# Second-half loads on ScalarE's queue, and a longer planned time for P's turn, in an attention and MLP kernel

## Chip, cores and metric

The kernel runs on one core of a Trainium2 chip. The metric is the device time of one execution in microseconds (us). A core has five engines that run side by side, each through a fixed list of instructions in order: TensorE (PE: matmuls), VectorE (DVE), ScalarE (ACT), GpSimd (POOL) and SyncE (SP), which here only issues DMAs. They meet through semaphores. 16 DMA engines move the data that any of them asks for.

## What is computed

Causal attention with a decay per head (4 batches, 8 heads, 576 positions, head width 64), then two MLPs on the 2,304 tokens (width 512; inner widths 2,048 and 1,536), all in float32:

```
scores = scale * np.matmul(q, k.transpose(0, 1, 3, 2))
cum = np.cumsum(np.log(np.clip(f, 0.0001, 1.0)), axis=-1)
scores = np.where(causal, -1000000000.0, scores + cum[:, :, :, None] - cum[:, :, None, :])
attn = np.exp(scores - np.max(scores, axis=-1, keepdims=True))
attn = attn / (np.sum(attn, axis=-1, keepdims=True) + 1e-09)
x = np.matmul(attn, v)        # then (tokens, 512)
r = np.maximum(x @ w_in, 0.0)
x = (r * r) @ w_out
g = x @ w_gate
out = (g * (1.0 / (1.0 + np.exp(-g))) * (x @ w_val)) @ w_out2
```

## The kernel before

**How the work is cut.** Precision comes from splitting each operand into a high and a low part and adding three (in the MLPs) or two matmuls. The attention runs in units: one unit is a batch `b` and a pair of heads `pr`, and does a half of the query rows (`attn_unit`, L343). The first half (`half` 0, "early") has the query rows 0 to 255 of all 16 units, in two tiles of 128 rows; the second half has rows 256 to 575 in three tiles, `i` = 4 (64 rows of both heads together), 3 and 2. Keys go up to 256 in the first half and to 576 in the second. The tokens of the first half make the MLP's token tiles 0 to 3 (256 tokens each, one for each batch), those of the second half tiles 4 to 8, laid end to end: 320 tokens a batch, so that tile 7 takes tokens of the batches 2 and 3, and tile 8 of batch 3 alone (`segments`, L869).

**A unit.** DMAs load K (`load_k`, L377), Q, V and the decay sums (`load_bias`, L395, broadcast to 128 partitions). ScalarE and VectorE split K and Q into parts (L402 to L418). For each tile and head (or both heads) TensorE makes the scores (L535), GpSimd masks the diagonal of the decay (L523), VectorE subtracts the decay and takes the row's extreme (`soft`, L558), ScalarE exponentiates (L576), and VectorE (with ScalarE for one of the two heads) writes P's high and low part as fp16 (L605 to L611). Then SyncE issues *P's turn* (`turn`, L628 to L636): a transposing DMA (L633) that writes P with keys on the partitions. n = `ng * 2 * nb` blocks of 128 x 128 are turned: 10, 16 and 12 in the second half's tiles, 8 and 4 in the first half's. The value matmuls (`mix`, L649) read the turned P, ScalarE scales and keeps the result (L675), and the unit's rows are stored (L692).

**Buffers.** In the second half, K's load has one buffer (`kr`), the decay has one in each of two sets that alternate between units, P has two (`P16`) and the turned P two (`PT`). The first half has three of P and three of the turned P.

**The order of the work.** A planner (class `Plan`, L47) writes the order of each engine by hand. Every step has an engine, an estimated time, steps that it waits for, buffers that it takes and a priority. `Plan.order` (L65) runs the steps through a model: each engine starts the ready step of the smallest priority number whose buffers are free. An attention step has the priority 10 x the number of its unit, a matmul of an MLP 500 and up, and the MLP's steps on ScalarE, VectorE and GpSimd -100; so TensorE does attention when it can and MLP matmuls otherwise. The order found this way is what each engine runs on the chip; times on the chip don't change it. For a step on SyncE the model adds a transfer: 290,000 bytes for each us on one shared channel, then 1.8 us until it has landed (L103 to L106). P's turn stands in it with 1.4 us of issue and 250,000 bytes whatever its size (L636).

```
                if e == SP:
                    free[e] = now + st.us
                    dma_free = max(free[e], dma_free) + st.nbytes / DMA_RATE
                    st.done = dma_free + DMA_LATENCY
```

**Stages.** The first half of the attention runs beside the loading and splitting of the first MLP's weights and its token tiles 0 and 1; the second half beside the tiles 2 to 6 of the first MLP as they come free; then follow the rest of the first MLP (`mlp_pair`, L771, with `first`, L736, and `second`, L744) and the second MLP (`mlp_wide`, L999). All DMAs, loads, turns and stores, are issued by SyncE on one queue.

Of the kernel before, what the change touches and what calls it, by code (L numbers as in the profile page):

```python
# [10 lines left out]
F16 = mybir.dt.float16  # L11
# [6 lines left out]
PE, ACT, DVE, POOL, SP = "PE", "ACT", "DVE", "POOL", "SP"  # L18
AFTER = {PE: 0.25, ACT: 0.2, DVE: 0.15, POOL: 0.2, SP: 0.0, None: 0.0}
DMA_ISSUE = 0.45  # L20
DMA_LATENCY = 1.8
DMA_RATE = 290e3
LAG1 = 2
GATE = 1
PACE = 4
LAG2 = 1

# [19 lines left out]
class Plan:  # L47
# [6 lines left out]
        first.next.append((then, False))  # L54


    def add(self, eng, us, fn, deps=(), pri=0, take=(), use=(), nbytes=0, order=()):
        deps, order = ([d for d in ds if d is not None] for ds in (deps, order))
        st = Step(len(self.steps), eng, us, fn, deps, order, pri, take, nbytes)
        for buf in (*take, *use):  # L60
            buf.users.append(st)
        self.steps.append(st)
        return st

    def order(self):  # L65
        now, dma_free = 0.0, 0.0
        free = {e: 0.0 for e in AFTER}
        cands = {e: [] for e in AFTER}
        rings, events, left = {}, [], len(self.steps)

        def fits(st):
            more = {}
            for buf in st.take:
                ring = rings.setdefault(buf.tag, [])
                at = len(ring) + more.get(buf.tag, 0) - buf.n
                more[buf.tag] = more.get(buf.tag, 0) + 1
                if at >= 0:
                    for u in ring[at].users:
                        if u.start is None or u.done > now:
                            return False  # L80
            return True

        for st in self.steps:
            if not st.left:
                cands[st.eng].append(st)
        while left:
            moved = False
            for e in free:
                if free[e] > now and e is not None:
                    continue  # L90
                best = None
                for st in cands[e]:
                    if st.ready <= now and (best is None or (st.pri, st.idx) < (best.pri, best.idx)) and fits(st):
                        best = st
                if best is None:
                    continue
                moved, st = True, best
                cands[e].remove(st)
                left -= 1
                st.start = now  # L100
                for buf in st.take:
                    rings[buf.tag].append(buf)
                if e == SP:  # L103
                    free[e] = now + st.us
                    dma_free = max(free[e], dma_free) + st.nbytes / DMA_RATE
                    st.done = dma_free + DMA_LATENCY  # L106
                else:
                    free[e] = now + st.us
                    st.done = now + st.us + AFTER[e]
                heapq.heappush(events, free[e])  # L110
                heapq.heappush(events, st.done)
                for nx, wait in st.next:
                    nx.left -= 1
                    nx.ready = max(nx.ready, st.done if wait else st.start)
                    if not nx.left:
                        cands[nx.eng].append(nx)
            if moved:
                continue
            while events and events[0] <= now:
                heapq.heappop(events)  # L120
            if not events:
                stuck = [st for e in cands for st in cands[e]]
                raise RuntimeError(f"the plan is stuck at {now}: {[(s.eng, s.pri, s.fn, [b.tag for b in s.take]) for s in stuck[:8]]}")
            now = heapq.heappop(events)
        return sorted(self.steps, key=lambda st: (st.start, st.idx))
# [22 lines left out]
def decay_attention_moe_kernel(ctx: ExitStack, tc, q, k, v, f, w1, w2, wg, wv, wo, outT):  # L148
    nc = tc.nc
    P = 128  # L150
# [36 lines left out]
    add = plan.add  # L187
# [36 lines left out]
    decayed = add(SP, DMA_ISSUE, lambda: nc.sync.dma_start(cum_d, fc[0]), [o3], -10, use=[fc_buf], nbytes=74000)  # L224
# [118 lines left out]
    def attn_unit(idx, b, pr, half, opened):  # L343
# [16 lines left out]
        c = {}  # L360
        x_buf = c["xbuf"] = XBUF[b] if early else None

        def take(eng, us, fn, deps, bufs, use=(), nbytes=0, p=pri):
            st = add(eng, us, fn, [*deps, opened], p, take=bufs, use=use, nbytes=nbytes,
                     order=[prev(x.tag) for x in bufs])
            for x in bufs:
                alloc_chain[x.tag] = st
            return st
# [8 lines left out]
        def load_k():  # L377
            if early:
                c["kr"] = h0.tile([P, 2, SPLIT], F32, tag="qk", bufs=3, name="kr")
            else:  # L380
                c["kr"] = pool().tile([P, 2, S], F32, tag="kr", name="kr")[:, :, :kmax]
            nc.sync.dma_start(c["kr"], k[b, h2, :, :kmax].rearrange("h d s -> d h s"))

        cols = slice(pr * P, pr * P + P)

# [9 lines left out]
        def load_bias():  # L395
            c["bias"] = kq_pool().tile([P, 2, kw], F32, tag="bias", bufs=nbuf, name="bias")
            r0 = b * H + 2 * pr
            nc.sync.dma_start(
                c["bias"][:, :, :kmax], cum_d[r0 : r0 + 2, :kmax].partition_broadcast(P)
            )  # L400

# [19 lines left out]
            (Buf("qk", 3), Buf("qk", 3)) if early else (Buf("kr", 1), Buf("qr", 1))  # L421
        ) + (Buf(tg + "vr", nbuf), Buf(kt + "bias", nbuf))
        KA, QA = Buf(kt + "KA", nbuf), Buf(kt + "QA", nbuf)
        lk = take(SP, DMA_ISSUE, load_k, [], [kr], nbytes=P * 8 * kmax)
        lq = take(SP, DMA_ISSUE, load_q, [], [qr], nbytes=P * 8 * qn)
        lb = BIAS[idx] = take(SP, DMA_ISSUE, load_bias, [decayed], [bias], nbytes=P * 8 * kmax)
        lv = take(SP, DMA_ISSUE, load_v, [], [vr], nbytes=P * 4 * 512)
        lv2 = add(SP, DMA_ISSUE, load_v2, [lv], pri, use=[vr], nbytes=32000)
        lv3 = add(POOL, 0.27, lambda: nc.gpsimd.memset(c["vr"][64:128, TAIL, :], 0.0), [lv], pri, use=[vr])
# [71 lines left out]
        for ti, i in enumerate(tiles):  # L501
# [86 lines left out]
                nc.vector.reciprocal(cg[:, :, 3], cg[:, :, 3])  # L588

            sm = add(DVE, 0.32, sums, exps, pri, use=[cg_buf])  # L590
            p_buf, t_buf = Buf(tg + "P16", 3 if early else 2), Buf(tg + "PT", 3 if early else 2)
            lows, pad = [], None
            for g in range(ng):
                on_act = early or g == 1

                def view(st=st, g=g, ng=ng, nb=nb):
                    return st["p16"].rearrange("p (g a n) -> p g a n", g=ng, a=2)[:, g]

                def p_hi(st=st, g=g, ng=ng, nb=nb, ext=ext, on_act=on_act, view=view):
                    if g == 0:  # L600
                        p16 = pool().tile([P, (8 if early else 16) * P], F16, tag="P16", bufs=3 if early else 2, name="p16")
                        st["p16"] = p16[:, : ng * 2 * nb * P]
                    cg, s, pv = st["cg"][:, g], st["s", g], view()
                    if on_act:
                        nc.scalar.activation(pv[:, 0, :ext], s[:, :ext], AF.Copy, scale=cg[:, 3:4])  # L605
                    else:
                        nc.vector.tensor_scalar(pv[:, 0, :ext], s[:, :ext], cg[:, 3:4], None, op0=ALU.mult)

                def p_lo(st=st, g=g, ext=ext, view=view):
                    cg, s, pv = st["cg"][:, g], st["s", g], view()  # L610
                    nc.vector.scalar_tensor_tensor(  # L611
                        pv[:, 1, :ext], s[:, :ext], cg[:, 3:4], pv[:, 0, :ext],
                        op0=ALU.mult, op1=ALU.subtract,
                    )

                eng, us = (ACT, act_us(ext)) if on_act else (DVE, dve1_us(ext))
                if g == 0:
                    first_hi = ph = take(eng, us, p_hi, [sm], [p_buf], use=[sbufs[g], cg_buf])
                else:
                    ph = add(eng, us, p_hi, [sm, first_hi], pri, use=[p_buf, sbufs[g], cg_buf])  # L620
                lows.append(add(DVE, dve_us(ext), p_lo, [ph], pri, use=[p_buf, sbufs[g], cg_buf]))
                if ext < nb * P:
                    lows.append(add(
                        POOL, 0.3, lambda view=view, ext=ext: nc.gpsimd.memset(view()[:, :, ext:], 0.0),
                        [ph], pri, use=[p_buf],
                    ))

            def turn(st=st, ng=ng, nb=nb):  # L628
                PT = pool().tile(
                    [P, (8 if early else 16) * P], F16, tag="PT", bufs=3 if early else 2, name="PT"  # L630
                ).rearrange("p (n q) -> p n q", q=P)
                n = ng * 2 * nb
                nc.sync.dma_start_transpose(out=PT[:, :n, :], in_=st["p16"])  # L633
                st["PT"] = PT[:, :n, :].rearrange("p (g a b) q -> p g a b q", g=ng, a=2)

            tn = take(SP, 1.4, turn, lows, [t_buf], use=[p_buf], nbytes=250000)  # L636


            def mix(ps, st=st, i=i, nb=nb, w=w):
# [539 lines left out]
```

## Time and profile before

| | us |
|---|---|
| median of 3 runs | 1107.16 (1103.6 to 1111.46) |
| the profiled execution | 1107.47 |
| its span, first to last instruction | 1105.7 |
| TensorE busy | 1028.4 |
| VectorE busy | 568.3 |
| ScalarE busy | 548.8 |
| GpSimd busy | 250.9 |

The profile is of one execution. An engine counts as busy while an instruction of its own runs on it; issuing a DMA, waiting and branching are not counted. "PE" is TensorE's matmuls and "PEld" its weight loads, which overlap them. Matmuls overlap one another, so a row's duration is longer than the distance to the next. "PEclk" is the share of TensorE's full clock (2.4 GHz) that was granted; 0.50 is the lower level, 1.2 GHz. A wait is named by who waited and by what ended it; "DMA PT<-p" is the landing of a turn of P. For a DMA, "to landing" is the time from the start of its issue until its data is there.

### The profile page before, as it was taken

To read this page: it belongs to the slowest core of one execution; us is meant where nothing else is said; L and a number is where in the kernel's file an instruction comes from. 1 tells how busy PE (TensorE), PEld (TensorE's weight loads), DVE (VectorE), ACT (ScalarE), POOL (GpSimd) and SP (SyncE) were. 2 spreads that over 40 slices of the span, in tenths; PEclk is the share of its full clock that TensorE was granted. 3 is DMA by queue.
4 is the path that set the end of the run, shared out by engine and by line. 5 is a ranking of instruction groups with operands and counts; after the bars stand their busy time and mean duration, and the time that the engine had idled before them with its cause. 6 is when DMAs were issued, how large, how long until landed. Compare 5 with 4: busy or idle time off the path is not lost.

```text
span 1105.7 us, 20516 instructions
## 1 busy us (share of the span) xinstructions
PE 1028.4 (93%) x7936; PEld 924.7 (84%) x7936; DVE 568.3 (51%) x1239; ACT 548.8 (50%) x1104; POOL 250.9 (23%) x341
## 2 busy tenths in 40 slices
PE   2567999999889998989999999999999999999998
PEld 2457999998889888979999998888888888888897
DVE  7889988537668878767371899102002000100010
ACT  6877888756556666756573887112112111211111
POOL 1232432332223223222122211111111111111111
PEclk9997999999889999989999999999999999999999
DMA  9978357459798979776561555002001100100010
GB/s 322 259 163 253 100 153 172 77 153 213 169 196 207 201 184 225 164 169 125 150 198 43 160 167 180 0 1 77 1 1 29 48 1 1 39 1 1 1 39 20
DMA packets 177922, 128.89 MB, mean 117 GB/s; under 512 B 110944, under 2 KB 164704, under 8 KB 176032
## 3 DMA queue, kind: packets, MB, share of 16 engines
q1 hardware_dynamic: 177824, 127.58, 45.2%
q8 instruction: 62, 1.02, 0.4%
q14 instruction: 36, 0.29, 0.1%
HBM read 89.20 MB, written 12.13 MB: 92 GB/s over the span
## 4 chain that ended last, share of the span: by engine, by line
PE 79%; DMA 10%; DVE 7%; issue 2%; ACT 2%; POOL 0%; SPq 0%; POOLq 0%; DVEq 0%; ACTq 0%
PE hp L739 29%; PE acc L747 16%; PE vp L739 14%; PE acc L1058 12%; DMA PT<-p 9%; PE ps L649 4%; PE ps L535 4%; DVE p L611 1%; DVE s L558 1%; DVE ct L270 1%; DVE ct L276 1%; DVE QB L410 1%; DMA raw<-in_moe_w_in_dram 1%; DVE wl_i L285 1%; DVE ct L266 0%
## 5 line engine op out<-in xcount | busy, mean ns | idle before, releaser
L1030 DVE TENSOR_TENSOR tmp<-tmp,vp 128x512 f32<-128x512 f32 x48 | 33.0, 687 | 301.9 <-PE vp L739 301.9
L825 POOL TENSOR_TENSOR gl<-tmp,gh 128x512 fp32r<-128x512 f32 x78 | 113.8, 1459 | 295.2 <-ACT gh L822 287.5
L739 PE MATMUL hp<-xh,wh_i 128*128 128x256 f32 x576 | 168.4, 292 | 0.0
L747 PE MATMUL acc<-gh,wh_o 128*128 128x256 f32 x576 | 166.1, 288 | 0.0
L739 PE MATMUL hp<-xl,wh_i 128*128 128x256 f32 x576 | 165.5, 287 | 0.0
L739 PE MATMUL hp<-xh,wl_i 128*128 128x256 f32 x576 | 165.2, 287 | 0.0
L747 PE MATMUL acc<-gh,wl_o 128*128 128x256 f32 x576 | 164.0, 285 | 1.2 <-DVE wl_o L285 1.2
L747 PE MATMUL acc<-gl,wh_o 128*128 128x256 f32 x576 | 164.1, 285 | 0.0
L1037 POOL TENSOR_TENSOR gl<-tmp,gh 128x512 fp32r<-128x512 f32 x48 | 62.6, 1304 | 335.5 <-ACT gh L1034 335.5
L739 PEld LDWEIGHTS hp<-xh,wh_i 128*128 128x128 f32 x576 | 112.9, 196 | 2.6 <-issue 0.7
L739 PEld LDWEIGHTS hp<-xl,wh_i 128*128 128x128 f32 x576 | 113.0, 196 | 0.6
L747 PEld LDWEIGHTS acc<-gh,wh_o 128*128 128x128 f32 x576 | 111.1, 193 | 2.1 <-ACT KA L414 0.2
L739 PEld LDWEIGHTS hp<-xh,wl_i 128*128 128x128 f32 x576 | 112.5, 195 | 0.0
L747 PEld LDWEIGHTS acc<-gh,wl_o 128*128 128x128 f32 x576 | 111.3, 193 | 1.5 <-DVE wl_o L285 1.5
L747 PEld LDWEIGHTS acc<-gl,wh_o 128*128 128x128 f32 x576 | 111.3, 193 | 0.7
L523 POOL TENSOR_SCALAR_AFFINE_SELECT bias<-bias 128x128 f32<-128x128 f32 (+1 forms) x160 | 66.1, 420 | 188.9 <-DVE cg L558 99.3
L1027 ACT ACTIVATE tmp<-hp 128x512 f32<-128x512 f32 x48 | 28.6, 596 | 160.2 <-PE hp L739 158.2
L576 ACT ACTIVATE s<-s,cg 128x256 f32<-128x256 f32 (+4 forms) x144 | 83.4, 579 | 40.5 <-DVE cg L558 40.0
L649 PE MATMUL ps<-PT,VT 128*64 128x128 f16 (+2 forms) x1920 | 69.2, 225 | 33.1 <-DMA PT<-p 24.6
L558 DVE CUSTOM_DVE_ANT_0 s<-ps,bias 128x512 f32<-128x512 f32 (+3 forms) x160 | 76.2, 481 | 41.8 <-PE ps L535 26.7
L649 PEld LDWEIGHTS <-VT 128*64 128x64 f16 (+1 forms) x1920 | 56.1, 117 | 46.3 <-DMA PT<-p 32.9
L611 DVE SCALAR_TENSOR_TENSOR p<-s,cg,p 128x256 f16<-128x256 f32 (+4 forms) x144 | 91.2, 650 | 6.8 <-ACT p L605 5.3
(99 smaller groups left out, 2362.7 us busy)
## 6 DMA issues: line engine op xcount, KB each, us to landing
kr<-in_k_dram SPq DMA_DIRECT2D x16, 576.0 KB, 5.9
bias<-cum_d SPq DMA_DIRECT2D x16, 576.0 KB, 5.6
vr<-in_v_dram SPq DMA_DIRECT2D x32, 256.0 KB, 3.5
raw<-in_moe_w_in_dram SPq DMA_DIRECT2D x8, 1024.0 KB, 5.8
raw<-in_moe_w_out_dram SPq DMA_DIRECT2D x16, 512.0 KB, 4.4
xm<-x_d SPq DMA_DIRECT2D x14, 512.0 KB, 4.2
raw<-in_moe_w_out_dram SPq DMA_DIRECT2D x6, 1024.0 KB, 6.9
raw<-in_moe_w_gate_dram SPq DMA_DIRECT2D x12, 512.0 KB, 4.1
```

Source lines behind the costliest of these rows:

```text
L523: nc.gpsimd.affine_select(diag, diag, pattern=[[-1, w]], compare_op=ALU.is_ge, fill=-8e9, base=0, channel_multiplier=1,)
L535: nc.tensor.matmul(ps[:M, : n1 - n0], c["Q"][j][:, h, qc - q0 : qc - q0 + M], c["K"][:, h, n0:n1], start=j == 0, stop=j == 1,)
L558: nc.vector.tensor_tensor_reduce(out=s[r0:r1, n0:e1], in0=c[key][r0:r1, : e1 - n0], in1=c["bias"][r0:r1, h, n0:e1], scale=-0.125, scalar=3 ...
L576: nc.scalar.activation(s[:, :ext], s[:, :ext], AF.Exp, bias=cg[:, mc : mc + 1], scale=-1.0, accum_out=cg[:, 2:3],)
L611: nc.vector.scalar_tensor_tensor(pv[:, 1, :ext], s[:, :ext], cg[:, 3:4], pv[:, 0, :ext], op0=ALU.mult, op1=ALU.subtract,)
L649: nc.tensor.matmul(ps[64 * h : 64 * h + 64, :w], c["VT"][:K, blk, h, va, :], rhs, start=(blk == 0 and a == 0 and va == 0), stop=(blk == nb ...
L739: nc.tensor.matmul(ps, w[wi][:, kk, c * P : (c + 1) * P], x[xi][:, kk, :], start=(kk == 0 and (wi, xi) == (0, 0)), stop=(kk == KC - 1 and ...
L747: nc.tensor.matmul(acc[:, d, :], w[wi][:, c, d * P : (d + 1) * P], g[gi][:, u, :], start=(st and d % 2 == 0 and (wi, gi) == (0, 0)), stop= ...
L825: nc.gpsimd.tensor_tensor(G[k0][2], G[k0][0], G[k0][1].bitcast(F32), op=ALU.subtract)
L1030: nc.vector.tensor_tensor(G[k0][0], G[k0][0], HP.pop(k1), op=ALU.mult)
L1037: nc.gpsimd.tensor_tensor(G[k0][2], G[k0][0], G[k0][1].bitcast(F32), op=ALU.subtract)
L1058: nc.tensor.matmul(A[2, j][half][:, d - part[0], :], W["f", m // 4][wi][:, m % 4, d * P : (d + 1) * P], G[k0][1 + gi], start=(m == 0 and ( ...
```

## The change

In the second half, the loads of K and of the decay are issued by ScalarE instead of SyncE, and stand in the plan as ScalarE's steps (`far`). The model of a transfer now applies to every step with bytes, on whichever engine. P's turn is planned with bytes that grow with its size (1.6 x 32,768 for a block) and lands 3.0 us later than other transfers in the plan (`late`); this holds for both halves. P has three buffers in the second half too. No step is added or taken away, and the arithmetic is the same.

```diff
+TURN_COST = 1.6
+TURN_LATE = 3.0
...
-    def add(self, eng, us, fn, deps=(), pri=0, take=(), use=(), nbytes=0, order=()):
+    def add(self, eng, us, fn, deps=(), pri=0, take=(), use=(), nbytes=0, order=(), late=0.0):
...
+        st.late = late
...
-                if e == SP:
+                if st.nbytes:
                     free[e] = now + st.us
                     dma_free = max(free[e], dma_free) + st.nbytes / DMA_RATE
-                    st.done = dma_free + DMA_LATENCY
+                    st.done = dma_free + DMA_LATENCY + st.late
...
-            nc.sync.dma_start(c["kr"], k[b, h2, :, :kmax].rearrange("h d s -> d h s"))
+            (nc.sync if early else nc.scalar).dma_start(c["kr"], k[b, h2, :, :kmax].rearrange("h d s -> d h s"))
...
-            nc.sync.dma_start(
+            (nc.sync if early else nc.scalar).dma_start(
                 c["bias"][:, :, :kmax], cum_d[r0 : r0 + 2, :kmax].partition_broadcast(P)
             )
...
-        lk = take(SP, DMA_ISSUE, load_k, [], [kr], nbytes=P * 8 * kmax)
+        far = SP if early else ACT
+        lk = take(far, DMA_ISSUE, load_k, [], [kr], nbytes=P * 8 * kmax)
         lq = take(SP, DMA_ISSUE, load_q, [], [qr], nbytes=P * 8 * qn)
-        lb = BIAS[idx] = take(SP, DMA_ISSUE, load_bias, [decayed], [bias], nbytes=P * 8 * kmax)
+        lb = BIAS[idx] = take(far, DMA_ISSUE, load_bias, [decayed], [bias], nbytes=P * 8 * kmax)
...
-            p_buf, t_buf = Buf(tg + "P16", 3 if early else 2), Buf(tg + "PT", 3 if early else 2)
+            p_buf, t_buf = Buf(tg + "P16", 3), Buf(tg + "PT", 3 if early else 2)
...
-                        p16 = pool().tile([P, (8 if early else 16) * P], F16, tag="P16", bufs=3 if early else 2, name="p16")
+                        p16 = pool().tile([P, (8 if early else 16) * P], F16, tag="P16", bufs=3, name="p16")
...
+            n_turn = ng * 2 * nb
...
-            tn = take(SP, 1.4, turn, lows, [t_buf], use=[p_buf], nbytes=250000)
+            tn = take(SP, 1.4, turn, lows, [t_buf], use=[p_buf], nbytes=TURN_COST * n_turn * 32768, late=TURN_LATE)
```

## Rows read from the trace of the kernel before

**Rows 1.** The page: the span, busy time of the engines, TensorE in 40 slices
```profile
span 1105.7 us, 20516 instructions
...
PE 1028.4 (93%) x7936; PEld 924.7 (84%) x7936; DVE 568.3 (51%) x1239; ACT 548.8 (50%) x1104; POOL 250.9 (23%) x341
...
PE   2567999999889998989999999999999999999998
```

**Rows 2.** Windows by stage: stretch, its us, busy us (instructions), clock, DMA share, GB/s
```profile
0.00:245.00 245.00, 195.58 (x1652) 181.07 (x1653) 192.73 (x488) 187.14 (x417) 72.84 (x120) 0.97 0.69 185
245.00:532.00 287.00, 264.48 (x3137) 248.81 (x3136) 215.51 (x520) 179.87 (x378) 79.60 (x147) 0.96 0.81 181
532.00:648.00 116.00, 116.00 (x957) 115.48 (x956) 69.79 (x100) 78.93 (x139) 28.13 (x20) 1.00 0.48 146
```

**Rows 3.** TensorE's waits, 245 to 532 us: total us, times, longest
```profile
PE ps L649 <- DMA PT<-p: 20.6, 12, 4.9
```

**Rows 4.** TensorE in order of time: start, us, instruction, [idle before it]
```profile
292.54 1.92 PE L649 MATMUL ps<-PT,VT 128*64 128x128 f16 x32 [2.72 <-DMA PT<-p]
...
295.20 0.41 PE L739 MATMUL hp<-xh,wh_i 128*128 128x256 f32 x1
```

**Rows 5.** Windows, the stretch behind that wait; clock is third from the end
```profile
291.40:298.20 6.80, 5.66 (x49) 5.49 (x50) 1.37 (x5) 0.84 (x2) 2.50 (x5) 0.50 1.05 238
```

**Rows 6.** The line of P's turn, 245 to 532 us: ns minimum/median/maximum, and landing
```profile
L633 SPq DMA_TRANSPOSE PT<-p x48: 1261/1961/4168, 245.1 to 523.8; - x48
...
DMA to landing us min/median/max: 3.3/4.3/9.7
```

**Rows 7.** SyncE in order of time, 468 to 480 us
```profile
469.57 0.58 SPq L398 DMA_DIRECT2D bias<-cum_d  x1
...
470.72 0.41 SPq L375 DMA_DIRECT2D qr<-in_q_dram  x1
471.23 8.58 SPq L633 DMA_TRANSPOSE PT<-p  x2
```

**Rows 8.** The turn issued at 471.23 us: who waited for it, and its landing
```profile
  PE ps L649: 4.9, 1
...
DMA to landing us min/median/max: 9.7/9.7/9.7
```

**Rows 9.** SyncE in order of time: the last store of the attention
```profile
531.73 0.34 SPq L692 DMA_DIRECT2D x_d<-U  x1
```

**Rows 10.** TensorE's groups by line, 531.8 to 648 us: first MLP, count, busy us, mean ns
```profile
L747 PE MATMUL acc<-gh,wh_o 128*128 128x256 f32 x160 | 45.3, 283 | 0.0
...
L739 PE MATMUL hp<-xh,wl_i 128*128 128x256 f32 x156 | 44.1, 283 | 0.0
...
L739 PE MATMUL hp<-xl,wh_i 128*128 128x256 f32 x155 | 43.9, 283 | 0.0
```

**Rows 11.** The chain that ended last, merged: start, us, line and count
```profile
642.36 2.88 PE acc L747 x24
```

**Rows 12.** SyncE's waits, 245 to 532 us
```profile
SPq L633 <- DVE p L611: 82.9, 41, 8.2
...
SPq L382 <- DVE KA L418: 4.1, 3, 2.5
...
SPq L398 <- DVE cg L558: 2.0, 4, 1.0
```

**Rows 13.** VectorE's waits, 245 to 532 us
```profile
DVE p L607 <- DMA PT<-p: 3.1, 3, 1.3
```

**Rows 14.** The lines of K's and the decay's loads, 245 to 532 us: ns minimum/median/maximum
```profile
L382 SPq DMA_DIRECT2D kr<-in_k_dram x14: 367/384/1275, 249.7 to 470.2; - x14
...
L398 SPq DMA_DIRECT2D bias<-cum_d x14: 353/556/1273, 255.0 to 489.7; - x14
```

**Rows 15.** ScalarE's waits, 245 to 532 us
```profile
ACT s L576 <- DVE cg L558: 28.5, 25, 2.9
```

**Rows 16.** The line of P's turn, 0 to 245 us: who waited (us, times)
```profile
  PE ps L649: 4.0, 4
```

More of the change, by code (lines that the diff above doesn't have):

```diff
@@ L361, in attn_unit, with take @@
         x_buf = c["xbuf"] = XBUF[b] if early else None
-        def take(eng, us, fn, deps, bufs, use=(), nbytes=0, p=pri):
-            st = add(eng, us, fn, [*deps, opened], p, take=bufs, use=use, nbytes=nbytes,
+        def take(eng, us, fn, deps, bufs, use=(), nbytes=0, p=pri, late=0.0):
+            st = add(eng, us, fn, [*deps, opened], p, take=bufs, use=use, nbytes=nbytes, late=late,
                      order=[prev(x.tag) for x in bufs])
```

## The prediction

> **What bounds the kernel now.** I read the page first [rows 1]: TensorE is busy for 93% of the span, VectorE for 51%, so TensorE's work is the floor, and what a change can win is TensorE's idle time and the time at its lower clock. The line of slices puts the holes in the first four slices and in a stretch from slice 9 to 18. The windows by stage [rows 2] give their sizes. From 0 to 245 us (first half of the attention) TensorE idles 49.4 us, nearly all before 100 us, while VectorE and ScalarE feed it. From 245 to 532 us (second half of the attention, the stage that the change edits) it idles 287.0 - 264.5 = 22.5 us and the mean granted clock is 0.96. From 532 us on it has no hole worth a term.
>
> Next I ask what ended each wait in the second stage. Of those 22.5 us, 20.6 us in 12 pieces, the longest 4.9 us, were ended by one thing: the landing of a turn of P (the transposing DMA that the value matmuls read) [rows 3]. The clock belongs to the same holes. Behind the wait that ended at 292.54 us the 256-column matmuls take 0.41 us instead of the stage's usual 0.28, and from 291.4 to 298.2 us the granted clock is 0.50, the 1.2 GHz level [rows 4, 5]. The mean of 0.96 over 287 us is 0.04 x 287 = 11.5 us lost that way. Price of the late turns in this stage: 20.6 + 11.5 = 32.1 us.
>
> Why are turns late? One lands 3.3 us after its issue at best, 4.3 in the median, 9.7 at worst [rows 6]. The worst shows how: the decay (bias), K and Q loads are issued from 469.57 us on, the turn right behind them at 471.23 us on the same queue, and it lands 9.7 us later; the wait it ends is the 4.9 us one [rows 7, 8]. The old planner gives a turn 1.4 us of issue, 250,000/290,000 = 0.86 us of transfer and 1.8 us of latency, 4.06 us if the queue is empty. So half of the turns land later than planned, and TensorE, which runs in a fixed order, stands before the value matmuls.
>
> **The turn's time in the plan.** The new cost is 1.4 + 1.6 x n x 32,768/290,000 + 1.8 + 3.0 us for n blocks. The three tiles of a second-half unit have n = 10, 16 and 12: 8.01, 9.09 and 8.37 us, that is 3.95, 5.03 and 4.31 us more. No instruction is added; the value matmuls move back in TensorE's order and filler (matmuls of the first MLP) moves in front. The longest wait, 4.9 us, is about the new slack, the other eleven are shorter, so by arithmetic all 20.6 us go, and with no hole the clock has no cause shown here to fall.
>
> But moving filler forward only helps if there is filler. Behind the last store of the attention, at 531.73 us [rows 9], come 480 matmuls of the MLP's second product (three groups of 160) and 466 of its first (156 + 155 + 155) [rows 10]. One token tile takes 16 x 12 x 2 = 384 of them. Tiles 7 and 8 need the last batch's attention and can't move: 768. So 946 - 768 = 178 matmuls can, at 2.88/24 = 0.12 us each [rows 11]: 21.4 us. If the attention stage keeps its 287 us, this is the gain. To win all of the 32.1 us the stage would have to shorten by 10.7 us.
>
> **Does the stage keep its length?** A turn starts when VectorE has written P: SyncE waited for that 41 times, 82.9 us in all [rows 12]. Three times VectorE in turn waited for a landing before it could write P, 3.1 us in all [rows 13]: the two P buffers. The third buffer removes that, and is needed, since a turn planned at 9 us holds P for longer; it costs SBUF and no instruction. There are still two buffers for the turned P. Held for 8.49 us (mean of the three) plus 1.41 us for the value matmuls in the plan's own figures, two of them allow a tile each 4.95 us, against 287/48 = 5.98 us now. That fits unless the plan's DMA queue adds over 2.06 us a turn. I take no change of the length; the ends are 10.7 us shorter and, by the queue part below, 13.2 us longer.
>
> **The loads on ScalarE's queue.** SyncE gives up 16 loads of K and 16 of the decay; I put that at nothing by itself, since a turn's issue waits for VectorE anyway [rows 12]. ScalarE gets 32 issues. The trace has none on ScalarE; the nearest rows are SyncE's of the same loads, 0.384 and 0.556 us in the median, 1.275 at most [rows 14]: 16 x 0.384 + 16 x 0.556 = 15.0 us, of which 14/16 = 13.2 us stand in this window, at least 28 x 0.35 = 9.8, at most 28 x 1.275 = 35.7 us. ScalarE is busy 179.9 of the 287 us [rows 2], so 107 us of idle time can hide them; I cost them at nothing, at 13.2 us if they all stand on the chain (by the median, the row to which most of them are nearest). Each load waits for its buffer: K for VectorE's split of the K before (SyncE waited 4.1 us, 3 times, on it), the decay for the last softmax pass of an older unit (2.0 us, 4 times) [rows 12]. Queued behind it on ScalarE are the exponentials, then VectorE's P, then the turn. But ScalarE already waits 28.5 us for the same softmax passes [rows 15], so most of that wait isn't new.
>
> What a second queue does to the transfers themselves I bound from turns: between landing behind the loads (9.7 us) and as if alone (3.3 us) [rows 6, 8]. The trace of before has only one queue for data, so it doesn't show which. I take the present median for most turns, inside the planned 8 to 9 us. On this the Trainium skill speaks against the change. Its page "DMA: Bandwidth & Descriptors" (section "Issuing engines are not separate DMA queues") says that loads from another engine run on the same 16 DMA engines and save only the issue time; by it alone this part is worth nothing, which is what the sum has. Its section "Queues, rings and completion order" adds that a DMA engine takes turns between queue rows; then loads issued behind a turn can delay it too, which is the third rival. No run here yet shows it.
>
> **The first half.** The constants apply there too (n = 8 and 4: 3.59 and 2.86 us more), while loads stay where they are. Four waits on turns cost TensorE 4.0 us [rows 16]; against that, the first MLP tile may start up to 3.6 us later. Between -4.0 and +3.6 us I take 0, since the start is fed by VectorE.
>
> **Sum.** The profiled execution took 1107.47 us (span 1105.7, 1.8 outside it), the median is 1107.16: the same. 1107.5 - 21.4 = **1086 us**. Its own range: 1107.5 - 32.1 - 4.0 = 1071 to 1107.5 - 21.4 + 13.2 = 1099 us.
>
> **Rivals.** 1. *The ring of turned P sets the pace.* If the planned queue (K and decay of a unit are 1.18 MB, 4.1 us at the planner's rate, put ahead of one turn) makes a buffer's hold 12.5 us instead of 9.9, a tile takes 6.25 us, the stage 300 us, 13 longer, and filler runs out near its end: 1107.5 + 13 - 21.4 = 1099 us, a gain under 1%. For it: the DMA share is already 0.81 in this stage [rows 2]. Against: real turns land in half the planned time.
>
> 2. *ScalarE's queue blocks (slower).* Every load at the maximum, 35.7 us, with none hidden, on the chain score, exponential, P, turn: 1107.5 - 21.4 + 35.7 = 1122 us. It decides from 21.4 us of unhidden issue on. For it: ScalarE runs in order and a load ahead of an exponential holds it up. Against: 107 us of idle time, and the loads have the lowest priority there.
>
> 3. *The turns get slower with their allowance.* If two queues share the engines so that the 28 turns near loads land after 9.7 us, they miss the planned 8.0 to 9.1 us by 0.6 to 1.7 us, 28 x 1.2 = 33 us of late landings. With the filler already used up to 21.4, the time is 1107.5 - 21.4 + 20 (about as much as TensorE waits now) = 1106 us: no change.
>
> **How the numbers follow.** Forecast 0.64, rival 1 0.14, rival 2 0.12, rival 3 0.10. One per cent, 11 us, is about what a measurement of this kernel tells from no change (its three runs lie within 8 us). Faster by over 1% (under 1096 us) holds most of the forecast and a little of rival 1: 0.65. Within 1%: the forecast's tail, rivals 1 and 3 and the mild cases of rival 2: 0.24. Slower: 0.11. The range for 8 in 10 goes from 1071, the forecast's lower end, past rivals 1 and 3 to 1111 us; rival 2 in full is left out.
>
> **What would show it.** Right: in the second stage TensorE's waits for turns fall from 20.6 to under 5 us, the clock there is 0.99 or 1.00, the MLP behind the attention is down to some 92 us, and turns still land in 4 to 6 us. Rival 1: waits on turns gone, but the last store comes later than 545 us. Rival 2: ScalarE's waits for softmax passes or for K's split grow, and VectorE waits for exponentials. Rival 3: turns land 8 us and later and still end TensorE's waits. The forecast is wrong if the waits on turns go and the time stays: then they were cover for VectorE's chain of softmax passes, which would appear as TensorE's waits for scores or P.

## The result, and the profile after

| | before | after |
|---|---|---|
| median, us | 1106.54 (1103.6 to 1111.46, 4 runs) | 1092.51 (1091.03 to 1093.51, 4 runs) |
| the profiled execution | 1107.47 | 1093.29 |
| its span | 1105.7 | 1091.2 |
| last store of the attention, start | 531.73 | 524.97 |

The ratio after to before is 0.9868 (95% interval 0.9829 to 0.9906): 14 us, or 1.3%, faster. The forecast was 1086 us, a gain of 21.4. The 6.5 us between 1086 and 1092.5 are the small part of the story: behind the 14 us stand a gain of 23 us from one half of the change and a loss of some 10 us from the other. One execution of the runs below (1161.12 us, in run 2) fell into a slow state of the chip, and no time or ratio here uses it.

The page of the changed kernel, the lines of [rows 1] and what is new in it:

```profile
span 1091.2 us, 20455 instructions
...
PE 1025.8 (94%) x7936; PEld 920.2 (84%) x7936; DVE 572.5 (52%) x1239; ACT 551.6 (51%) x1104; POOL 263.2 (24%) x341
...
PE   3478999997997999999999999999999999999998
...
PEclk9998999999998999999999999999999999999999
...
kr<-in_k_dram ACTq DMA_DIRECT2D x16, 576.0 KB, 5.5
bias<-cum_d ACTq DMA_DIRECT2D x16, 576.0 KB, 4.4
```

The matmuls are the same 7,936, so what changed is idle time and the clock. A slice is 27.3 us. Of the second stage, slices 10 and 13 show a 7, and the others from 9 to 20 a 9: most of the idle time that is left (12.7 of 14.0 us) lies from 246 to 273 us and from 327 to 355 us. The same windows as in [rows 2]:

```profile
0.00:245.00 245.00, 198.94 (x1685) 184.19 (x1686) 196.11 (x491) 192.92 (x424) 74.47 (x122) 0.98 0.70 186
245.00:532.00 287.00, 272.97 (x3223) 255.44 (x3223) 215.46 (x517) 181.75 (x377) 92.13 (x147) 0.98 0.88 185
```

From 245 to 532 us TensorE is busy for 8.5 us more than before and its mean clock is 0.98 instead of 0.96. It isn't the 0.99 or 1.00 forecast. What TensorE still waits for in this stretch (answers to [rows 3]):

```profile
PE ps L655 <- DMA PT<-p: 7.0, 3, 3.6
PE ps L539 <- ACT U L681: 3.3, 4, 1.3
PE ps L655 <- DVE cg L562: 2.3, 4, 1.7
PE ps L539 <- DVE cg L562: 1.2, 3, 0.7
```

The landings of turns cost 7.0 us instead of 20.6, in three pieces instead of twelve. And the turns themselves (answers to [rows 6]):

```profile
L639 SPq DMA_TRANSPOSE PT<-p x47: 1253/1998/8286, 248.1 to 514.1; - x47
...
DMA to landing us min/median/max: 3.4/4.9/15.0
```

They land no earlier than before: the median went from 4.3 to 4.9 us and the worst from 9.7 to 15.0. Seven of them take over 8 us, where before one did. So TensorE doesn't wait less because P is turned sooner; it waits less because the order no longer puts it before the turns. The seven long ones are new, and the three waits that are left belong to three of them (issued at 248.14, 253.84 and 333.25 us). The first is easily followed. SyncE in order of time, with the load of Q that stands ahead of the turn:

```profile
246.81 0.38 SPq L378 DMA_DIRECT2D qr<-in_q_dram  x1
248.14 2.99 SPq L639 DMA_TRANSPOSE PT<-p  x1
...
253.84 5.00 SPq L639 DMA_TRANSPOSE PT<-p  x1
```

ScalarE in the same stretch issues a load of the decay 0.7 us behind the first turn:

```profile
248.82 0.34 ACTq L401 DMA_DIRECT2D bias<-cum_d  x1
```

That turn, with who waited for it and its landing:

```profile
  PE ps L655: 3.6, 1
...
DMA to landing us min/median/max: 12.8/12.8/12.8
```

It takes 12.8 us, the load beside it 11.7 us (the last line of its answer), against a median of 4.3 us for the 14 loads of that line. TensorE pays twice, first with idle time, then with the clock, as in [rows 4, 5]:

```profile
260.99 1.92 PE L655 MATMUL ps<-PT,VT 128*64 128x128 f16 x32 [3.59 <-DMA PT<-p]
```

```profile
260.70:264.10 3.40, 3.11 (x38) 2.94 (x39) 1.09 (x2) 0.97 (x2) 1.96 (x5) 0.50 1.26 181
```

The second row is the window behind that wait; the granted clock is 0.50, the 1.2 GHz level.

**Where the 14 us come from.** Two stretches make the span: up to the last store of the attention, and the MLP work behind it. The store answers to [rows 9]:

```profile
524.97 0.34 SPq L698 DMA_DIRECT2D x_d<-U  x1
```

It comes 531.73 - 524.97 = 6.8 us earlier. Behind it, the first MLP's matmuls (answers to [rows 10], but counted up to 700 us; there are three groups like each of these):

```profile
L753 PE MATMUL acc<-gh,wl_o 128*128 128x256 f32 x166 | 47.0, 283 | 0.0
...
L745 PE MATMUL hp<-xh,wh_i 128*128 128x256 f32 x144 | 40.8, 283 | 0.0
```

These are 3 x 166 + 3 x 144 = 930. In the kernel before, the same count up to 700 us is larger than the 946 of [rows 10], which end at 648 us; one of its three groups of the second product, in the same view:

```profile
L747 PE MATMUL acc<-gh,wl_o 128*128 128x256 f32 x176 | 49.8, 283 | 0.0
```

So it was 3 x 176 + 466 = 994. At 0.12 us each [rows 11] the difference of 64 is 7.7 us. Together 6.8 + 7.7 = 14.5 us, which is the difference of the spans, 1105.7 - 1091.2. Half of the gain is a shorter stage, half is filler that moved forward.

### The profile page after: what moved, and what is told of

The parts are those of the page before. It is cut to its first block, busy times and chain, and to the rows that moved or that the text cites. A ratio compares the mean times of both kernels' runs of the same rounds, so it can differ in the third digit from the quotient of the medians.

```text
span 1091.2 us, 20455 instructions
## 1 busy us (share of the span) xinstructions
PE 1025.8 (94%) x7936; PEld 920.2 (84%) x7936; DVE 572.5 (52%) x1239; ACT 551.6 (51%) x1104; POOL 263.2 (24%) x341
## 4 chain that ended last, share of the span: by engine, by line
PE 78%; DVE 10%; DMA 5%; issue 4%; ACT 2%; SPq 0%; POOL 0%; DVEq 0%; ACTq 0%; POOLq 0%
PE hp L745 28%; PE acc L753 16%; PE vp L745 14%; PE acc L1064 12%; PE ps L539 4%; PE ps L655 4%; DVE s L562 1%; DVE p L615 1%; DMA vr<-in_v_dram 1%; DVE KA L421 1%; DMA PT<-p 1%; DMA x_d<-tmp 1%; DMA bias<-cum_d 1%; DVE ct L273 1%; DVE ct L279 1%
## 5 line engine op out<-in xcount | busy, mean ns | idle before, releaser
L527 POOL TENSOR_SCALAR_AFFINE_SELECT bias<-bias 128x128 f32<-128x128 f32 (+1 forms) x160 | 78.7, 499 | 205.0 <-DVE cg L562 118.1
L615 DVE SCALAR_TENSOR_TENSOR p<-s,cg,p 128x256 f16<-128x256 f32 (+4 forms) x144 | 91.7, 647 | 13.7 <-ACT p L609 12.3
L539 PE MATMUL ps<-KA,QA 128*128 128x256 f32 (+2 forms) x192 | 71.3, 375 | 25.5 <-DVE cg L562 13.1
L1040 ACT CAST gh<-tmp 128x512 fp32r<-128x512 f32 x48 | 29.8, 620 | 125.4 <-DVE tmp L1036 125.4
```

The source lines that it names most:

```text
L527: nc.gpsimd.affine_select(diag, diag, pattern=[[-1, w]], compare_op=ALU.is_ge, fill=-8e9, base=0, channel_multiplier=1,)
L539: nc.tensor.matmul(ps[:M, : n1 - n0], c["Q"][j][:, h, qc - q0 : qc - q0 + M], c["K"][:, h, n0:n1], start=j == 0, stop=j == 1,)
L615: nc.vector.scalar_tensor_tensor(pv[:, 1, :ext], s[:, :ext], cg[:, 3:4], pv[:, 0, :ext], op0=ALU.mult, op1=ALU.subtract,)
```

## Experiments

The runs take the change apart into its two halves, and then look at each half. Ratios are to the kernel before, timed beside each run (its medians lay between 1104.9 and 1106.8 us, 1105.6 for the first three); brackets are 95% intervals. "Long" is a turn of over 8 us.

**1. The plan alone.** The loads go back to SyncE, in the plan too; the turn's new cost and the third P buffer stay.

```diff
-            (nc.sync if early else nc.scalar).dma_start(c["kr"], k[b, h2, :, :kmax].rearrange("h d s -> d h s"))
+            nc.sync.dma_start(c["kr"], k[b, h2, :, :kmax].rearrange("h d s -> d h s"))
...
-            (nc.sync if early else nc.scalar).dma_start(
+            nc.sync.dma_start(
...
-        far = SP if early else ACT
+        far = SP
```

> The changed kernel with K's and the decay's loads back on SyncE's queue (longer planned turn and third P buffer kept). Theory A (the plan makes the gain; a turn and a load in flight together on two queues slow each other, which is why turns of 10 to 15 us appear in the changed kernel): as fast as the changed kernel or faster, 1080 to 1093 us, no turn over 10 us, TensorE's waits for turns in the second stage under 5 us. Theory B (the second queue is needed so that turns don't stand behind loads): waits for turns come back, 1096 to 1105 us.

Measured: 1082.37 us, ratio 0.9793 [0.9769, 0.9818]; 23 us faster than before and 10 us faster than the whole change (some 8 by the ratios, whose intervals don't meet). Its second stage as a window, TensorE's waits there, its turns and its last store:

```profile
245.00:532.00 287.00, 281.57 (x3317) 264.70 (x3317) 223.15 (x534) 191.41 (x398) 100.72 (x149) 0.99 0.90 195
```

```profile
PE ps L539 <- DVE cg L562: 3.4, 3, 2.2
PE ps L655 <- DVE cg L562: 1.1, 2, 0.8
PE ps L539 <- ACT U L681: 0.5, 1, 0.5
```

```profile
DMA to landing us min/median/max: 3.4/4.9/8.1
```

```profile
510.74 0.34 SPq L698 DMA_DIRECT2D x_d<-U  x1
```

No wait for a turn is left, and the median landing is the 4.9 us of the whole change, so the plan and not the queue took these waits away, as theory A has it. The last store comes 531.73 - 510.74 = 21.0 us earlier. The MLP matmuls behind it are 970, 24 fewer than before (2.9 us): 21.0 + 2.9 = 23.9 us, against 1105.7 - 1081.7 = 24.0 us of span. The gain of the plan is a shorter stage; hardly any filler moved.

**2. The queue alone.** The loads on ScalarE; the turn planned as before, two P buffers.

```diff
-            p_buf, t_buf = Buf(tg + "P16", 3), Buf(tg + "PT", 3 if early else 2)
+            p_buf, t_buf = Buf(tg + "P16", 3 if early else 2), Buf(tg + "PT", 3 if early else 2)
...
-            tn = take(SP, 1.4, turn, lows, [t_buf], use=[p_buf], nbytes=TURN_COST * n_turn * 32768, late=TURN_LATE)
+            tn = take(SP, 1.4, turn, lows, [t_buf], use=[p_buf], nbytes=250000)
```

> The kernel before with K's and the decay's loads on ScalarE's queue, alone (old planned turn, two P buffers in the second half). Theory A: no gain, 1103 to 1115 us, TensorE's waits for turns 20 us or more in the second stage, some turns over 10 us. Theory B: a good part of the gain, 1093 to 1100 us, and fewer turns that land after 6 us.

Measured: 1143.67 us, ratio 1.0349 [1.0322, 1.0375], 38 us slower than before. Theory A's "no gain" holds, but the time is far past its 1115 us: a loss of that size was not foreseen. TensorE's waits for turns and the turns' landings, from 245 us to the end of the attention at 569 us:

```profile
PE ps L655 <- DMA PT<-p: 45.2, 18, 9.0
```

```profile
DMA to landing us min/median/max: 3.3/4.9/13.6
```

Six turns are long. With the plan's allowance and the third P buffer a second queue costs 10 us, without them 38. The four corners in us: before 1106, plan 1082, queue 1144, both 1093.

**3. Both, with two P buffers.**

```diff
-            p_buf, t_buf = Buf(tg + "P16", 3), Buf(tg + "PT", 3 if early else 2)
+            p_buf, t_buf = Buf(tg + "P16", 3 if early else 2), Buf(tg + "PT", 3 if early else 2)
...
```

> The changed kernel with two P buffers in the second half instead of three. If the third buffer is needed for the longer planned turn (held for 9 us and more, 6.5 us a tile with two): the second stage gets longer, 1098 to 1110 us, VectorE waits for landings before it writes P. If it isn't: within 5 us of the changed kernel, 1088 to 1098 us.

Measured: 1120.3 us, ratio 1.0144 [1.0107, 1.0182]: 28 us slower than the whole change, slower even than before, and 10 us past the range that was expected if the buffer is needed. VectorE's waits in the second stage:

```profile
DVE p L615 <- ACT p L609: 39.7, 15, 5.4
...
DVE p L611 <- DMA PT<-p: 9.3, 5, 3.4
```

VectorE waits 9.3 us for landings before it can write P (3.1 in [rows 13]), and 39.7 us for the high part of P that ScalarE writes (line 609), which was 6.8 us in the whole change. My reading is that with two buffers the planned hold of 8 to 9 us a turn leaves no room, so that P is written late and in lockstep. Why ScalarE's part comes late, by the P buffer itself or by the place that the plan gives it, the trace doesn't separate.

**4. The plan alone, with two P buffers**: run 1 with the edit of run 3.

> The version with the loads on SyncE's queue and two P buffers. If the third buffer is needed by the planned time itself: 1098 to 1112 us, as with the loads on ScalarE. If two buffers hurt only together with the second queue: 1080 to 1092 us.

Measured: 1093.48 us, ratio 0.9885 [0.9854, 0.9916], 11 us slower than run 1 and between the two ranges: the buffer is needed by the planned time itself, but by less than beside the second queue. The same waits:

```profile
DVE p L615 <- ACT p L609: 23.6, 13, 3.8
...
DVE p L611 <- DMA PT<-p: 5.2, 4, 1.9
```

The third buffer is worth 11 us where turns land within 8.6 us (the worst here), 28 where some take 13.

**5. The kernel before, with the third P buffer and nothing else.**

> The kernel before with the third P buffer alone. If it only serves the longer planned turn: within 6 us of the kernel before, 1100 to 1112 us. If it has a gain of its own: 1090 to 1100 us.

Measured: 1104.71 us, ratio 0.9991 [0.9972, 1.001]. By itself the buffer does nothing that the interval tells from zero; with the longer planned turn it is worth the 11 us of run 4.

**6. Run 1 with the first half's turns planned as before.**

```diff
-            tn = take(SP, 1.4, turn, lows, [t_buf], use=[p_buf], nbytes=TURN_COST * n_turn * 32768, late=TURN_LATE)
+            tn = take(SP, 1.4, turn, lows, [t_buf], use=[p_buf], nbytes=250000 if early else TURN_COST * n_turn * 32768, late=0.0 if early else TURN_LATE)
```

> The version with the loads on SyncE's queue and the longer planned turn in the second half alone (first half planned as before). If the gain is the second stage's: within 4 us of the run with both, 1079 to 1087 us. If the first half's plan gave a part: 1088 us or more.

Measured: 1085.24 us, ratio 0.9809 [0.9778, 0.9841]. Between the medians the first half's share is 2.9 us, by the ratios 1.8; the interval overlaps with that of run 1, so it isn't told from none.

**7 and 8. Which part of the turn's new cost?** Run 1 with `TURN_LATE = 0.0` (bytes by size alone), and run 1 with `nbytes=250000, late=TURN_LATE` (3.0 us later alone).

> The version with the loads on SyncE's queue, where the plan gives a turn its bytes by size but not the 3.0 us more. The slack of the second stage's turns falls from 4 to 5 us to 1 to 2 us. If the slack against landing is what counts: waits for turns come back in part (5 to 15 us) and the time is 1088 to 1100 us. If the size in the plan's queue is what counts: within 4 us of the version with both.

> The complement of the version without the 3.0 us: loads on SyncE's queue, three P buffers, a turn with the old 250,000 bytes whatever its size, but landing 3.0 us later in the plan. If slack before the value matmuls is all that counts, this is as good as the version with bytes by size (1076 to 1083 us). If the turn's size in the plan's shared channel does its own part (loads and turns kept apart): waits for turns stay at 5 us or more in the second stage and the time is 1086 us or more.

Measured: bytes by size alone 1078.8 us, ratio 0.9744 [0.9717, 0.977], the fastest version of all; 3.0 us alone 1088.52 us, ratio 0.986 [0.984, 0.9881]. TensorE's waits in the second stage, bytes by size alone:

```profile
PE ps L655 <- DMA PT<-p: 4.1, 3, 1.8
PE ps L539 <- DVE cg L562: 0.8, 3, 0.3
```

and 3.0 us alone:

```profile
PE ps L655 <- DVE cg L562: 3.3, 3, 2.5
PE ps L539 <- ACT U L681: 2.4, 1, 2.4
PE ps L539 <- DVE cg L562: 1.8, 5, 0.7
PE ps L655 <- DMA PT<-p: 1.0, 2, 0.9
```

The version that waits longer for turns is the faster one: its last store starts at 504.90 us, that of the other at 516.25. It waits for nearly nothing else (0.8 us), while the other waits 7.5 us for VectorE and ScalarE. So the waits for turns aren't all that the plan decides: the time of 3.0 us alone came out as its second case has it, but not by that case's cause, 5 us or more of waits for turns. (Run 1, with both, lies between at 1082.37; its interval just touches that of bytes alone.) A difference between the two entries that is certain: the bytes occupy the plan's one channel, and so move the transfers planned behind the turn as well, while the 3.0 us delay only those who need the turn. Of the 11 us between the two last stores, 5.2 are filler that the second version does ahead of its store (945 matmuls of the first MLP are left behind it, 988 in the other); which of the transfers makes the rest wasn't isolated. Bytes by size with the loads on ScalarE weren't tried either.

**9. DMAs alone and in pairs.** None of the reference's work; the turn of 16 blocks, the K load and the decay load, alone and two at a time, four times each.

```
def load_turn_one_queue():
    load_bias(nc.sync)
    turn(nc.sync)
def turn_bias_two_queues():
    turn(nc.sync)
    load_bias(nc.scalar)
```

> The disputed cost by itself; the kernel computes nothing of the reference: it only issues a turn of 16 blocks, K's load and the decay's load alone and in pairs, four times each, on one queue or on two, with the engines idle otherwise. Theory A: a turn on SyncE's queue with a load issued at the same moment on ScalarE's takes 9 to 13 us, both landing late, while the same pair on one queue is done after 5 to 7 us, and two loads on two queues after 5 us. Theory B: the pair on two queues takes no longer than on one queue, 5 to 7 us.

Measured to landing: a turn alone 4.2 to 4.4 us, the K load 3.7 to 3.9, the decay load 3.3 to 3.6. A turn behind the decay load on one queue 5.6 to 5.9 us. Issued at the same moment on two queues, the turn 5.9 to 6.3 us and the load 4.1 to 4.5. No pair comes near 12 us: theory B's 5 to 7 us hold, theory A's 9 to 13 are out.

**10. Pairs, the load some time after the turn.** As run 9, with the load behind the turn by six different delays; none of the reference's work.

```
def two_queues(cols):
    turn(nc.sync)
    later(cols)
    load_bias(nc.scalar)
```

> By itself again, and again without the reference's computation: a turn on SyncE's queue and a load that starts later, held back by VectorE copies of 64 to 3,456 columns, on the same queue or on ScalarE's. Theory A, mended after the pairs that were issued together took 6 us: the slow case is a load on the other queue that comes in while a turn is under way; for some delays between 0.3 and 3 us both land after 8 to 13 us, and never on one queue (under 7 us). Rival C: two DMAs in pairs never do this, all land under 7 us; then the long landings of the whole kernel need more than two DMAs in flight.

The turns' landings with both on SyncE's queue (12 turns), and then with the load on ScalarE's (24):

```profile
DMA to landing us min/median/max: 4.2/4.3/4.5
...
DMA to landing us min/median/max: 4.2/5.8/7.3
```

One queue: the later load costs the turn nothing. Two queues: up to 3 us, most when the load comes 0.9 us later. Still no 12 us: at these delays one load and one turn don't explain it (two of the turns, at 7.1 and 7.3 us, are just past the 7 of rival C).

**11. More in flight.** In the changed kernel a Q load stood ahead of the turn on SyncE's queue (246.81 us, ahead of the turn at 248.14). This run puts a load of Q's size and the turn on SyncE, and the decay load after a shorter or a longer delay, on either queue; further groups have the Q load behind the turn, or a second turn and the K load besides. None of the reference's work is done.

```
def q_turn(eng, cols):
    load_q()            # SyncE
    turn(nc.sync)
    later(cols)
    load_bias(eng)
```

> By itself once more, without the reference's computation: three or five DMAs in flight (a Q-sized load and a turn on SyncE's queue, or a turn and then the load, or a load, two turns, the decay's load and K's load); the decay's and K's loads come 0.3 or 1 us later, on the same queue or on ScalarE's. Rival C (a pair on two queues is harmless, but several DMAs behind one another on both queues are not): on two queues turns land after 10 us or more and the whole group is done later than on one queue by 2 us or more. If the groups on two queues are done as early as on one: what makes the 10 to 15 us in the whole kernel stays open.

The turn's line in three stretches of the group shown: all on one queue (33 to 55 us); the load issued on ScalarE's queue before the turn (59 to 80 us); the load on ScalarE's queue 0.6 us after the turn's issue (82 to 124 us):

```profile
L41 SPq DMA_TRANSPOSE pt<-p x3: 3004/3022/3148, 34.2 to 51.1; - x3
...
DMA to landing us min/median/max: 4.7/4.7/4.8
...
L41 SPq DMA_TRANSPOSE pt<-p x3: 4532/4617/4698, 59.4 to 74.5; - x3
...
DMA to landing us min/median/max: 6.6/6.7/6.8
...
L41 SPq DMA_TRANSPOSE pt<-p x3: 2609/2763/2942, 82.1 to 110.4; - x3
...
DMA to landing us min/median/max: 12.3/14.1/14.8
```

Here are the long turns, and the load beside them takes 11.5 to 14.0 us, as the 11.7 us in the changed kernel. Windows over one group of the slow case, and over one on a single queue (the last column is GB/s):

```profile
95.34:109.45 14.11, 0.63 (x3) 0.00 (x0) 1.00 0.90 102
...
42.60:49.72 7.12, 0.52 (x2) 0.00 (x0) 1.00 0.79 203
```

The same bytes at half the rate, while the engines count as busy 0.90 of the time. With five DMAs in flight and ScalarE's loads 0.6 us behind the first turn it is the same: that turn takes 15.1 to 16.9 us on two queues against 4.8 to 4.9 on one. The groups between lie between. Five in flight with ScalarE's loads begun 0.2 us ahead of the turn and 0.3 us behind it: 9.3 to 10.5 us. The Q load issued behind the turn instead of ahead of it, the decay load on ScalarE's queue 0.9 us after the turn: 9.0 to 9.4 us, and 4.3 to 4.4 on one queue. What inside the DMA engines does it no run here shows.

The kernels show the same meeting. In the changed kernel and in runs 2 and 3, twelve turns of the second stage take over 10 us. Seven of them were issued while another transfer of SyncE's queue was in flight and had a load of ScalarE's start 0.4 to 0.9 us behind them; the other five are each the next turn behind one of these seven. It isn't certain to happen: four more turns met a load in the same way, 0.3 to 0.9 us behind, and took 6.3 to 8.9 us.

**12. Both, but the loads on ScalarE wait for the last turn.** ScalarE reads a column of the newest turned P before each of the loads, so that none starts beside a turn issued before it.

```diff
+    def turn_landed():
+        if last_turn:
+            nc.scalar.copy(seen_turn, last_turn[-1])
...
+            if not early:
+                turn_landed()
...
```

> The changed kernel, where a load on ScalarE's queue waits until the turn issued last has landed (ScalarE reads one column of it first). Theory A: no turn over 10 us any more in the second stage, TensorE's waits for turns under 4 us; the time is 1082 to 1092 us if ScalarE's waiting is hidden, above the changed kernel's 1092 if not. Rival C or any other cause of the long landings: turns of over 10 us remain.

Measured: 1100.17 us, ratio 0.995 [0.9925, 0.9975]. Turns now land within 9.3 us, none over 10 us as theory A has it, and TensorE's waits for them are gone, so the overlap was what made turns that long in the kernel too. What replaced them, ScalarE's waits and then TensorE's:

```profile
ACT seen L350 <- DMA PT<-p: 25.9, 11, 6.6
```

```profile
PE ps L549 <- ACT U L693: 10.0, 6, 5.8
...
PE hp L757 <- ACT xh L736: 5.0, 1, 5.0
```

ScalarE runs in order; held up for 25.9 us ahead of its loads, it is late with what TensorE needs. This is the second rival's mechanism, made on purpose.

## Why the prediction was right and where it was wrong

**The bound** was read rightly. TensorE's idle time in the second stage and its low clock are what moved. Idle from 245 us to the last store: 22.5 us before, 14.0 after, 5.4 with the plan alone, 50.5 with the queue alone. The time at the 1.2 GHz level over the same stretch was 23.9 us before, 10.2 after and 6.8 with the plan alone, and TensorE was busy in 20.1, 9.6 and 6.3 us of it. At that level the 256-column matmuls start 0.21 us apart (behind the wait of the changed kernel above), else 0.12. If half of that busy time is lost, 22.5 + 10.0 = 32.5, 14.0 + 4.8 = 18.8 and 5.4 + 3.2 = 8.6 us are lost in all: gains of 13.7 and 23.9 by this estimate, against 14.2 and 23.6 between the profiled executions. The clock's part of it is the less certain one: over the whole kernel TensorE's busy time fell by only 2.6 us (1028.4 to 1025.8) and 4.3 us (to 1024.1), and idle time before 245 us by some 3 us in either version.

Of the signs named for being right, none came out in full with the whole change: waits for turns at 7.0 us (under 5), the clock at 0.98 (0.99 or 1.00), the MLP behind the attention at 112 us (92), seven turns past 8 us (4 to 6). With the plan alone the first two did.

**The turn's time in the plan.** "21.4 us" stands beside 23 measured (run 1), but by another way than its step, so that their closeness is luck. The step "I take no change of the length" failed: the stage became 21 us shorter, and filler hardly moved (24 matmuls of a supposed 178, itself a count cut off at 648 us: there are 994 behind the stage, and 994 - 768 = 226 that could move). The sign that went with it, an MLP of some 92 us behind the attention, came out as 930 x 0.12 = 112 us, and 116 in run 1. The error was to treat the stage as bound by something else, so that removed waits could only be filled. The runs show that it can shorten; how much of a gain is shorter stage and how much is moved filler differs with the planned order: 6.8 and 7.7 us in the whole change, 21.0 and 2.9 in run 1, 26.8 and 0.7 with bytes by size alone, 15.5 and 5.9 with the 3.0 us alone. The reading that goes with it is argued from the order and not shown: a wait of TensorE for a turn also delays the scores behind it in its fixed list, and with them the next softmax passes, P and turn, so that the waits were links of the stage's own chain. In run 1 the stage shortened by about their own 20.6 us, in the other versions not. The prediction had that case as its lower end, 10.7 us of shortening beside all the filler; it was 21.0 and nearly none.

**The third P buffer** "is needed" held: without it the plan's gain falls from 23 to 13 us (run 4), and alone it gives nothing (run 5). The ring of two turned-P buffers, rival 1, is not seen: the last store comes earlier, not after 545 us.

**Loads on ScalarE, their issue**, costed at nothing, held. In the changed kernel:

```profile
L401 ACTq DMA_DIRECT2D bias<-cum_d x14: 345/345/353, 248.8 to 474.3; - x14
...
L385 ACTq DMA_DIRECT2D kr<-in_k_dram x14: 374/374/704, 246.4 to 459.0; - x14
```

That is 14 x 0.345 + 14 x 0.374 = 10.1 us, near the lower end of 9.8 given for it, and ScalarE's wait for softmax passes rose only to 30.8 us from 28.5 [rows 15]. Rival 2 didn't occur in this change; run 12 shows what it looks like.

**Loads on ScalarE, the transfers.** This is the step that failed and made the difference to the forecast: "I take the present median for most turns, inside the planned 8 to 9 us". The median did hold (4.9 us), and most turns land in time. But seven land after 8.1 to 15.0 us, most of them past their allowance; the four over 10 us stand in two stretches, 248 to 269 and 333 to 348 us (the two slices with a 7), in each of which loads on ScalarE's queue started while a turn and other transfers of SyncE were under way. Most of the other loads met a turn without such harm; what turns start such a stretch is told under run 11. Price: 1092.5 - 1082.4 = 10 us. It is the third rival's mechanism at a part of its size (7 turns, not 28; 10 us, not 20), and its sign was in the first profile. The bound for it, 9.7 us from a turn behind loads on one queue [rows 8], was too low: no row of before had a second queue.

On the rule of the Trainium skill named in the prediction: in "DMA: Bandwidth & Descriptors", section "Issuing engines are not separate DMA queues", issuing from another engine saves only issue time. The runs agree that there is nothing to gain (plan alone beats both), and go further. If the engines only took turns between the queues, as its section "Queues, rings and completion order" has it, a turn of 4.7 us with a load of 3.3 to 3.6 us coming in beside it would by my estimate land by about 8.3 us; 12.3 to 14.8 us was measured (run 11).

**The first half** at 0 between -4.0 and +3.6 us: run 6 gives 2.9 us of gain between medians, within it and not told from 0. TensorE's idle time before 245 us is 46.9 us in run 1 and 47.3 in run 6.

**The sum.** 21.4 + 0 forecast; 23 - 10 measured, and 14 in the direct comparison.

## What to carry to other kernels

When an order is planned by hand, first make the planner's costs of transfers follow their size: here that, with a third P buffer, took 1106.8 us to 1078.8 without one instruction added, and 3.0 us of allowance on top made it no faster (1082.4). Waits inside a chain aren't filler slots: ask whether the waiting engine itself feeds what the stage waits for next, and if so, don't cap the gain at the filler that is left: here the stage itself shortened, by 6.8 to 26.8 us with the planned order. A second DMA queue isn't free even when its issuing engine has time: before moving loads, find out by a small run of the very DMAs that will meet, with all that is in flight there, what they do to each other.

## What the runs showed of the hardware that was not expected

A transposing DMA with another transfer ahead of it on one queue and a load that starts 0.6 us later on a second queue: both take 11.5 to 14.8 us, at 102 GB/s, against 4.7 us for the turn and 203 GB/s with all on one queue. The pair without the third transfer takes 7.3 us at most, and of the same three a load that starts ahead of the turn makes 6.7 us of it. With everything on one queue no turn of runs 9 to 11 took over 5.9 us. So what makes turns of 12 us and more here is several transfers in flight and a load of the second queue just behind the turn, not the second queue as such. It isn't the only way to a long turn: in the kernels with one data queue single turns took 9.7 us (before), 10.1 (run 7) and 10.5 (run 5). On one queue, a load issued behind a turn cost the turn nothing (4.3 us, as alone).
